# Feed-forward tiles in pairs, with their last passes on 64 rows each

## The chip, the core and the metric

The kernel runs on one core of a Trainium2 chip. The metric is the device time of one execution in microseconds, the median over several runs. The engines of the core are named as in the profile: PE multiplies matrices (PEld is its loading of weights), ACT applies functions, DVE and POOL do elementwise work, and SP issues most DMAs.

## The reference

The reference is one transformer block with modulated layer normalization, for 2048 tokens of 448 features in fp32: windowed attention with 16 heads, then a feed-forward network with the Mish function. Cut to what matters here:

```
h = _layernorm(x, axis=-1) * (1 + ca) + sa
x = x + ga * _A_ref(h, A_wqkv, A_wo)          # attention, window 256
h = _layernorm(x, axis=-1) * (1 + cb) + sb
x = x + gb * _B_ref(h, B_w1, B_b1, B_w2)

def _B_ref(x, w1, b1, w2):                    # w1: 448 x 1792, w2: 1792 x 448
    h = jnp.einsum("bsd,df->bsf", x, w1) + b1
    sp = jnp.log1p(jnp.exp(-jnp.abs(h))) + jnp.where(h > 0, h, jnp.zeros_like(h))
    act = h * jnp.tanh(sp)
    return jnp.einsum("bsf,fd->bsd", act, w2)
```

## The kernel before

The tokens are worked in four groups of 512 (NG = 4, GT = 512). Matmuls take fp32r operands, which PE streams faster than fp32 but with fewer bits. To keep precision each operand is split into a high part, rounded to fp32r, and a low part, the rest: `hh` and `hl` for the normalized input, `w13` and `w1l` for the first layer's weights, `ah` and `al` for the activations, `w2h` and `w2l` for the second layer's weights. A product is then high times high, high times low and low times high.

The 448 input features of the first layer are four chunks of partitions, three of 128 and one of 64. `passes` (L210) lists the matmuls of one output tile: three for each full chunk, and two for the last. In the last chunk the 64 features stand twice, on partitions 0 to 63 and again on 64 to 127 (`dup`, L222, copies them before the transposition). Its weights `w13[:, 3]` have the high part on partitions 0 to 63 and the low part on 64 to 127 (`split_lo`, L195, writes it there). So the tenth pass, `hh[:, 3]` with `w13[:, 3]`, makes high times high and high times low at once. The eleventh, `hl[:, 3]` with `w13[:, 3]`, makes low times high and, on the other 64 rows, low times low.

The feed-forward has 14 tiles of 128 hidden features (NF = 14) in each group, so n counts 56 tiles (NN). `f1_mm(n)` (L907) writes the 128 x 512 tile `z` in one PSUM bank with 11 passes of 512 columns. `f1_act(n)` (L917) makes t = Mish(z + b1) on ACT (L921), its high part `ah` on ACT (L922) and its low part `al` on DVE (L923). `ff2(n)` (L1091) multiplies them with the second layer's weights: for each of four token tiles three matmuls of 448 columns into one of four `acc` banks, 12 in all. After the 14th tile of a group it multiplies each bank with the gate on DVE (L1104), adds the residual (L1107) and stores the rows on SP.

The eight PSUM banks are two for `z`, four for `acc` and two for `tr`, which the transpositions of the next group's normalization use. `ftile` (L902) gives `ah` and `al` two buffers each and `t` one, in the pool `p1`. The pool `ff` holds the second layer's weights and the tiles that come in during the feed-forward.

The order is written out by hand in the loop of L1134. In round n it issues the passes and the activation of tile n, then `ff2(n - 1)`, so the second layer runs one tile behind the first. Tiles 0 and 1 are issued before the loop, in the attention's tail. `fill_step` (L1129) stands before and after `ff2`: it moves other work on by a step, first the rest of the attention's output and then, from the third tile of a group on, the normalization and transposition of the next group (`gen_x1_ln2`, L1110). In group 0 `pieces(n)` (L887) also splits the weights that come in. Before a new group starts, the rest of the fill work is issued.

Of the kernel before, what the change touches and what calls it, by code (L numbers as in the profile page):

```python
# [8 lines left out]
F32 = mybir.dt.float32  # L9
F32R = mybir.dt.float32r  # L10
# [5 lines left out]
NG, GT = 4, 512  # L16
NF = F // 128
# [34 lines left out]
def adaln_block(ctx: ExitStack, tc: tile.TileContext, x, wqkv, wo, w1, b1, w2, c, w_mod, out):  # L52
    nc = tc.nc
    PE, ACT, DVE, POOL = nc.tensor, nc.scalar, nc.vector, nc.gpsimd
# [3 lines left out]
    def dma(o, i):  # L58
        nc.sync.dma_start(o, i)

    def pool(name, side="left", space=None):
        kw = {} if space is None else {"space": space}
        cm = tc.tile_pool(name=name, bufs=1, reuse_waits="tile", side=side, **kw)
        st = ExitStack()
        return st.enter_context(cm), st
# [25 lines left out]
    def bank(tag, bufs, name):  # L91
        return PS[0].tile([128, 512], F32, name=name, tag=tag, bufs=bufs)
# [18 lines left out]
    for k in range(4):  # L111
        wmf = st0.tile([128, 2 * D], F32, name=f"wm01_{k}")
        t = wmf[0:112]
# [11 lines left out]
    for part in range(3):  # L125
        for ci in range(4):
            r0, r1 = ci * 128, min(ci * 128 + 128, D)
            for h in ((slice(0, 128),) if ci < 3 else (slice(0, 64), slice(64, 128))):
                t = wqs[ci][h]
# [80 lines left out]
    def passes(xh, xl, wh, wl):  # L210
        r = []
        for ci in range(3):
            r += [(xh[:, ci], wh[:, ci]), (xh[:, ci], wl[:, ci]), (xl[:, ci], wh[:, ci])]
        return r + [(xh[:, 3], wh[:, 3]), (xl[:, 3], wh[:, 3])]
# [48 lines left out]
    def new_T(key, pl):  # L263
        return (pl.tile([128, 4, GT], F32R, name=f"hh{key}", tag="hh"),
                pl.tile([128, 4, GT], F32R, name=f"hl{key}", tag="hl"))
# [59 lines left out]
    def flush():  # L325
        while later:
            later.pop(0)()
# [123 lines left out]
    hh, hl = HT[0] = new_T(0, mid)  # L451
# [67 lines left out]
    for i in range(2):  # L519
        t = att.tile([128, GT], F32, name=f"o2_{i}")  # L520
# [5 lines left out]
    def xr_tile(name):  # L526
        return mid.tile([128, 512], F32, name=name, tag="xr", bufs=3)
# [254 lines left out]
    FW = {}  # L782
    w2h, w2l, w2p, h2, x1 = {}, {}, {}, {}, {}
# [22 lines left out]
    def w1_hi(n):  # L806
        ci, c0 = W1[n]
        split_hi(w1p[n], FW["w13"][:, ci, c0:c0 + D], ACT)

    def w1_lo(n, eng):  # L810
        ci, c0 = W1[n]
        split_lo(w1p[n], FW["w13"][:, ci, c0:c0 + D], FW["w1l"][:, min(ci, 2), c0:c0 + D], ci, eng)
# [4 lines left out]
    def piece_load(i):  # L817
        if i < len(SEQ):
            (w2_dma if SEQ[i][0] == "w2" else w1_load)(SEQ[i][1])
# [58 lines left out]
    def w2_split(f):  # L878
        n = NF - 1 - f
        pl = FW["p1"] if f == 0 else FW["ff"]  # L880
        w2h[f] = (mid.tile([128, D], F32R, name=f"w2h{f}", tag="wo", bufs=7) if n < 7 else
                  pl.tile([128, D], F32R, name=f"w2h{f}"))
        w2l[f] = pl.tile([128, D], F32R, name=f"w2l{f}")
        ACT.activation(w2h[f], w2p[f], AF.Copy)
        (DVE if f < 1 else POOL).tensor_tensor(w2l[f], w2p[f], w2h[f].bitcast(F32), op=ALU.subtract)

    def pieces(f):  # L887
        for i, (kind, n) in enumerate(SEQ):
            if kind == "w2" and n == f:
                w2_split(n)  # L890
            elif kind == "w1" and (n - 4) // 2 == f:
                w1_hi(n)
                w1_lo(n, DVE if f < 1 else POOL)
            else:
                continue
            if "ff" in FW:
                piece_load(i + 6)

    NN = NG * NF
    ah, al, acc = {}, {}, {}  # L900

    def ftile(nm, n, dt=F32):  # L902
        return FW["p1"].tile([128, GT], dt, name=f"{nm}{n}", tag=nm, bufs=1 if nm == "t" else 2)

    zb = {}

    def f1_mm(n, tag, part=(0, 11)):  # L907
        g, f = divmod(n, NF)
        hh, hl = h2[g]
        fs = slice(f * 128, (f + 1) * 128)  # L910
        if part[0] == 0:
            zb[n] = bank(tag, 2, f"z{n}")
        ps = passes(hh, hl, FW["w13"][:, :, fs], FW["w1l"][:, :, fs])
        for m in range(*part):
            PE.matmul(zb[n], ps[m][1], ps[m][0], start=(m == 0), stop=(m == 10))  # L915

    def f1_act(n):  # L917
        f = n % NF
        ah[n], al[n] = ftile("ah", n, F32R), ftile("al", n, F32R)
        t = ftile("t", n)  # L920
        ACT.activation(t, zb[n], AF.Mish, bias=FW["b1c"][:, f:f + 1])  # L921
        ACT.activation(ah[n], t, AF.Copy)  # L922
        DVE.tensor_tensor(al[n], t, ah[n].bitcast(F32), op=ALU.subtract)  # L923
# [105 lines left out]
    for u in range(NU + 9):  # L1029
        s, k = divmod(u, 3)  # L1030
        g = s // H
# [12 lines left out]
        a = s + LEAD  # L1044
# [42 lines left out]
    ff, ff_s = pool("ff")  # L1087
    FW["ff"] = ff
    p1 = FW["p1"]

    def ff2(n):  # L1091
        g, f = divmod(n, NF)
        if f == 0:
            acc[g] = [bank("acc", 4, f"acc{g}_{t}") for t in range(4)]
        for t in range(4):
            ts = slice(t * 128, (t + 1) * 128)
            p = acc[g][t][:, 0:D]
            PE.matmul(p, ah[n][:, ts], w2h[f], start=(f == 0), stop=False)  # L1098
            PE.matmul(p, ah[n][:, ts], w2l[f], start=False, stop=False)  # L1099
            PE.matmul(p, al[n][:, ts], w2h[f], start=False, stop=(f == NF - 1))  # L1100
            if f == NF - 1:
                j = 4 * g + t
                y = xr_tile(f"yo{j}")[:, 0:D]
                DVE.tensor_tensor(y, p, gbn, op=ALU.mult)  # L1104
                for eng, a, b in (((DVE, 0, D),) if g < NG - 1 else ((POOL, 0, D),) if t < 3 else
                                  ((DVE, 0, 256), (POOL, 256, D))):
                    eng.tensor_tensor(y[:, a:b], y[:, a:b], x1[g][:, t, a:b], op=ALU.add)  # L1107
                dma(of[j * 128:(j + 1) * 128, :], y)

    def gen_x1_ln2(g):  # L1110
        if g > 1:
            x1_load(g, (ff, p1)[g % 2])
            yield
            yield
            yield

        def xn_tiles():
            t = mid.tile([128, 4, 512], F32, name=f"xn2_{g}", tag="on")
            return [t[:, i] for i in range(4)]
        yield from gen_ln2(g, ff, xn_tiles, "tr", 2)  # L1120
# [8 lines left out]
    def fill_step():  # L1129
        if fill is not None:  # L1130
            pipe.step()
            next(fill, None)
            flush()
    for n in range(NN + 1):  # L1134
        g, f = divmod(n, NF)
        if f == 0 and n:
            while fill is not None and next(fill, "END") != "END":
                pipe.step()
            fill = None
            while pipe.items:  # L1140
                pipe.step()
        if f == 2 and 0 < g < NG - 1:
            fill = gen_x1_ln2(g + 1)
        if 2 <= n < NN:
            f1_mm(n, "z")
            f1_act(n)
        if 0 < n < NF:
            pieces(n)
        if n:
            if n > 1:  # L1150
                fill_step()
            ff2(n - 1)
            for _ in range(1 + (g == 0) + (n == 1)):
                fill_step()
    for st in (ff_s, mid_s, cst_s, FW["s"], edge_s, psf_s):
        st.close()

# [22 lines left out]
```

## Time and profile before

| | |
|---|---|
| median of 3 runs | 718.31 us (717.83 to 719.37) |
| profiled execution | 719.96 us |
| its span on the core | 718.2 us |
| mean granted PE clock | 0.99 |
| matmul share of the span | 97% (4049 matmuls) |
| weight loads | 83% |
| DVE, ACT, POOL | 53%, 54%, 46% |
| first passes of z / last passes start | 414.4 us / 706.2 us |

Times in profile rows are microseconds from the start of the span. A row of the timeline has the start, the duration, the engine, the line, the operation, output and inputs with buffer numbers left out, and the count; what stands in brackets is idle time before it and who ended it. In a matmul's shape, 128*60 means weights of 128 rows (partitions) and 60 columns. The recorded duration of a matmul is longer than the distance to the next one, since matmuls are pipelined. So the distance between starts is what a matmul costs in a stream. A row that groups instructions has, behind the bar, the busy time in us and the mean duration in ns, then the idle time before them. A row of windows has the stretch, its length, and the busy time of the engine in it, then the granted clock, the DMA share and GB/s.

### The profile page before, as it was taken

What the parts mean: (1) busy time and instruction counts of PE and PEld (TensorE: products, weight loads), DVE (VectorE), ACT (ScalarE), POOL (GpSimd) and SP (SyncE); (2) the same over time, 40 slices, a digit from 0 to 9 for tenths busy, and PEclk for the clock granted to TensorE, in tenths of its full rate; (3) what the DMA queues carried; (4) which work ended last, traced back from release to release, by engine and by line L of the source; (5) the groups of instructions that cost most, each with busy time, mean ns of one, the idle gap of its engine ahead of it and who ended that gap; (6) DMA issues with size and microseconds to landing.
All of it is one profiled execution on the core that took longest, in us unless ns stands there. A gap on an engine that the chain in (4) does not pass through costs nothing.

```text
span 718.2 us, 12057 instructions
## 1 busy us (share of the span) xinstructions
PE 694.9 (97%) x4049; PEld 597.3 (83%) x4049; DVE 380.0 (53%) x1018; ACT 390.9 (54%) x740; POOL 327.0 (46%) x358
## 2 busy tenths in 40 slices
PE   8999999999999999999999899999999999999996
PEld 8777878788898888898887688888888888888885
DVE  5688657788555878656768642434323232322112
ACT  4538778768766768767868774243224222422221
POOL 6636778676666767666869744422010000000002
PEclk9999999999999999999999899999999999999999
DMA  7865763453761653744672165400200020001001
GB/s 215 257 211 178 251 204 122 148 158 125 212 207 50 203 166 88 230 137 137 216 223 75 52 216 157 116 1 2 102 1 1 4 99 1 0 7 45 0 1 51
DMA packets 48249, 83.86 MB, mean 117 GB/s; under 512 B 6142, under 2 KB 26348, under 8 KB 48188
## 3 DMA queue, kind: packets, MB, share of 16 engines
q1 hardware_dynamic: 47724, 83.10, 37.1%
q8 instruction: 32, 0.52, 0.3%
q14 instruction: 29, 0.24, 0.1%
q10 hardware_dynamic: 464, 0.00, 0.0%
HBM read 53.45 MB, written 29.36 MB: 115 GB/s over the span
## 4 chain that ended last, share of the span: by engine, by line
PE 72%; issue 11%; DVE 8%; DMA 4%; ACT 2%; POOL 1%; SPq 1%; POOLq 0%; DVEq 0%; ACTq 0%
PE z L915 15%; PE pv L740 9%; PE qk L314 8%; PE sA L678 5%; PE acc L1098 5%; PE acc L1100 5%; PE acc L1099 5%; PE sB L708 5%; PE wo L314 4%; PE qk_v L314 4%; PE sB L719 3%; DVE junk L680 3%; PE et L754 2%; DMA q<-mr 1%; DMA scr<-st 1%
## 5 line engine op out<-in xcount | busy, mean ns | idle before, releaser
L730 POOL TENSOR_TENSOR Pl<-P,Ph 128x512 fp32r<-128x512 f32 (+2 forms) x192 | 234.5, 1229 | 87.1 <-ACT Ph L723 49.4
L680 DVE CUSTOM_DVE_ANT_0 junk<-sA,mask 128x384 f32<-128x384 f32 (+2 forms) x256 | 135.2, 528 | 97.8 <-PE sA L678 89.5
L722 ACT ACTIVATE P<-sB 128x512 f32<-128x512 f32 (+2 forms) x192 | 109.8, 572 | 66.9 <-PE sB L719 61.7
L923 DVE TENSOR_TENSOR al<-t,ah 128x512 fp32r<-128x512 f32 x56 | 38.7, 692 | 199.7 <-ACT ah L922 199.7
L921 ACT ACTIVATE t<-z,b1c 128x512 f32<-128x512 f32 x56 | 38.5, 688 | 188.8 <-PE z L915 181.6
L723 ACT ACTIVATE Ph<-sB 128x512 fp32r<-128x512 f32 (+2 forms) x192 | 109.2, 569 | 0.0
L678 PE MATMUL sA<-k,q 84*128 84x384 f32 (+2 forms) x256 | 100.9, 396 | 2.2 <-DVE mx L680 1.5
L915 PE MATMUL z<-hhf,w 128*128 128x512 f32 x224 | 89.6, 400 | 0.0
L915 PE MATMUL z<-hlf,w 128*128 128x512 f32 x224 | 88.4, 395 | 0.0
L1098 PE MATMUL acc<-w2h,ah 128*128 128x448 f32 x224 | 82.0, 366 | 0.0
L1100 PE MATMUL acc<-w2h,al 128*128 128x448 f32 x224 | 81.7, 365 | 0.0
L1099 PE MATMUL acc<-w2l,ah 128*128 128x448 f32 x224 | 81.4, 364 | 0.0
L740 PE MATMUL pv<-Ph,v 128*60 128x256 f32 (+2 forms) x352 | 77.6, 295 | 3.6 <-DVE o L748 2.3
L740 PE MATMUL pv<-Pl,v 128*60 128x256 f32 (+2 forms) x352 | 74.4, 286 | 2.3 <-POOL Pl L730 2.3
L708 PE MATMUL sB<-q,k 86*128 86x256 f32 (+1 forms) x352 | 74.7, 286 | 1.4 <-DMA q<-mr 1.4
L915 PE MATMUL z<-hhf,w1l 128*128 128x512 f32 x168 | 66.3, 395 | 0.0
L708 PEld LDWEIGHTS sB<-q,k 86*128 86x128 f32 x352 | 62.4, 191 | 2.9 <-issue 1.2
L740 PEld LDWEIGHTS pv<-Ph,v 128*60 128x60 f32 x352 | 46.0, 135 | 18.0 <-ACT o L746 3.2
L719 PE MATMUL sB<-fdmask,identr 128*128 128x128 bf16 (+1 forms) x320 | 60.6, 255 | 0.0
L678 PEld LDWEIGHTS sA<-k,q 84*128 84x128 f32 x256 | 48.9, 192 | 8.5 <-DVE mx L680 5.9
L740 PEld LDWEIGHTS pv<-Pl,v 128*60 128x60 f32 x352 | 45.7, 133 | 11.0 <-POOL Pl L730 3.9
L1107 POOL TENSOR_TENSOR yo<-yo,x 128x448 f32<-128x448 f32 (+1 forms) x4 | 4.2, 1064 | 108.1 <-DVE yo L1104 108.1
(156 smaller groups left out, 1300.4 us busy)
## 6 DMA issues: line engine op xcount, KB each, us to landing
scr<-st SPq DMA_DIRECT2D x24, 512.0 KB
k<-scr SPq DMA_DIRECT2D x48, 252.0 KB
q<-scr SPq DMA_DIRECT2D x64, 168.0 KB
scr<-st SPq DMA_DIRECT2D x32, 256.0 KB
x<-x1d SPq DMA_DIRECT2D x10, 448.0 KB
xin<-in_A_x_dram SPq DMA_DIRECT2D x8, 448.0 KB
xr<-in_A_x_dram SPq DMA_DIRECT2D x16, 224.0 KB
x1d<-xr SPq DMA_DIRECT2D x16, 224.0 KB
```

Of the source, the lines that this page charges most:

```text
L314: PE.matmul(p, b, a, start=(n == 0), stop=(n == 10))
L678: PE.matmul(p[:, c0:384], q[0:84, t * 128:(t + 1) * 128], k[0:84, t * 128 + c0:t * 128 + 384], start=True, stop=True)
L680: DVE.tensor_tensor_reduce(out=junk[:, c0:384], in0=p[:, c0:384], in1=mask[:, c0:384], scale=1.0, scalar=-3.0e38, op0=ALU.add, op1=ALU.max ...
L708: PE.matmul(p[:, c:c + 128 * (t1 - t0)], k[:, jj * 128:(jj + 1) * 128], q[:, t0 * 128:t1 * 128], start=(n == 0), stop=False, skip_group_ch ...
L722: ACT.activation(P[:, c0:], p[:, c0:], AF.Exp, scale=SCALE)
L723: ACT.activation(Ph[u][:, c0:], p[:, c0:], AF.Exp, scale=SCALE)
L730: eng.tensor_tensor(Pl[u][:, a:b], Pt[u][:, a:b], Ph[u][:, a:b].bitcast(F32), op=ALU.subtract)
L740: PE.matmul(pv[0:60, t0 * 128:t1 * 128], V[j % NV][:, h, :], P[u][:, c:c + 128 * (t1 - t0)], start=(P is Ph and b == 0 and n == 0), stop=F ...
L915: PE.matmul(zb[n], ps[m][1], ps[m][0], start=(m == 0), stop=(m == 10))
L1098: PE.matmul(p, ah[n][:, ts], w2h[f], start=(f == 0), stop=False)
L1099: PE.matmul(p, ah[n][:, ts], w2l[f], start=False, stop=False)
L1100: PE.matmul(p, al[n][:, ts], w2h[f], start=False, stop=(f == NF - 1))
```

## The change

Group 0 keeps its order. In groups 1 to 3 the tiles are taken two at a time. `f1_pair(n)` issues the first ten passes of tile n and the first ten of tile n + 1, and then one matmul of 64 rows for each in place of the eleventh pass: `hl[0:64, 3]` with the high weights on partitions 0 to 63 for tile n, and `hl[64:128, 3]` with a copy of the high weights on partitions 64 to 127 for tile n + 1. They write different PSUM banks and use different halves of the array's rows. The term low times low of the last 64 features is no longer in the sum for these groups. Then come both activations, and after them the second layer of the two tiles of the round before, each with its fill steps.

The copy `w1x` is a new tile of 128 x 7 x 128 in the pool `ff`; one DMA on SP fills its partitions 64 to 127 with the high weights of the seven odd tiles, after group 0's last round is issued. `ftile` takes every second pair's `ah`, `al` and `t` from the pool `ff`, so there are four buffers of `ah` and `al` and two of `t` in all.

```diff
     def ftile(nm, n, dt=F32):
-        return FW["p1"].tile([128, GT], dt, name=f"{nm}{n}", tag=nm, bufs=1 if nm == "t" else 2)
+        pl = FW["ff"] if n >= NF and n // 2 % 2 else FW["p1"]
+        return pl.tile([128, GT], dt, name=f"{nm}{n}", tag=nm, bufs=1 if nm == "t" else 2)
...
-    for n in range(NN + 1):
+    w1x = ff.tile([128, NF // 2, 128], F32R, name="w1x")
+
+    def f1_pair(n):
+        hh, hl = h2[n // NF]
+        for m in (n, n + 1):
+            f1_mm(m, "z", (0, 10))
+        f = n % NF
+        PE.matmul(zb[n], FW["w13"][0:64, 3, f * 128:(f + 1) * 128], hl[0:64, 3], start=False, stop=True)
+        PE.matmul(zb[n + 1], w1x[64:128, f // 2], hl[64:128, 3], start=False, stop=True)
+        for m in (n, n + 1):
+            f1_act(m)
+
+    for n in range(NF):
+        if 2 <= n:
+            f1_mm(n, "z")
+            f1_act(n)
+        if n:
+            pieces(n)
+            if n > 1:
+                fill_step()
+            ff2(n - 1)
+            for _ in range(2 + (n == 1)):
+                fill_step()
+    odd = FW["w13"][0:64, 3].rearrange("p (a b c) -> p a b c", b=2, c=128)[:, :, 1]
+    dma(w1x[64:128].bitcast(F32), odd.bitcast(F32))
+    last = [NF - 1]
+    for n in range(NF, NN + 2, 2):
         g, f = divmod(n, NF)
-        if f == 0 and n:
+        if f == 0:
             while fill is not None and next(fill, "END") != "END":
                 pipe.step()
             fill = None
             while pipe.items:
                 pipe.step()
-        if f == 2 and 0 < g < NG - 1:
+        if f == 2 and g < NG - 1:
             fill = gen_x1_ln2(g + 1)
-        if 2 <= n < NN:
-            f1_mm(n, "z")
-            f1_act(n)
-        if 0 < n < NF:
-            pieces(n)
-        if n:
-            if n > 1:
-                fill_step()
-            ff2(n - 1)
-            for _ in range(1 + (g == 0) + (n == 1)):
-                fill_step()
+        if n < NN:
+            f1_pair(n)
+        for m in last:
+            fill_step()
+            ff2(m)
+            fill_step()
+        last = [n, n + 1]
```

## The prediction

> **What bounds the kernel now.** I read the page first (busy shares, the chain), then the matmul timeline of the feed-forward, then single rows for the prices.
>
> ```profile
> span 718.2 us, 12057 instructions
> PE 694.9 (97%) x4049; PEld 597.3 (83%) x4049; DVE 380.0 (53%) x1018; ACT 390.9 (54%) x740; POOL 327.0 (46%) x358
> ...
> PE z L915 15%; PE pv L740 9%; PE qk L314 8%; PE sA L678 5%; PE acc L1098 5%; PE acc L1100 5%; PE acc L1099 5%; PE sB L708 5%; PE wo L314 4%; PE qk_v L314 4%; PE sB L719 3%; DVE junk L680 3%; PE et L754 2%; DMA q<-mr 1%; DMA scr<-st 1%
> ```
>
> Matmul is busy nearly always, and the chain that ended last runs through the lines of the feed-forward. A busy matmul record is not a proof (each is longer than the distance to the next), so the stretch in which the last three groups run has to be looked at by itself.
>
> ```profile
> 494.00:704.00 210.00, 210.00 (x986) 1.00 0.06 23
> ...
> 703.91 0.39 PE L915 MATMUL z<-hhf,w 128*128 128x512 f32 x1
> 704.15 0.39 PE L915 MATMUL z<-hhf,w1l 128*128 128x512 f32 x1
> ...
> 706.01 0.39 PE L915 MATMUL z<-hhf,w 128*128 128x512 f32 x1
> 706.24 0.39 PE L915 MATMUL z<-hlf,w 128*128 128x512 f32 x1
> 706.47 0.37 PE L1098 MATMUL acc<-w2h,ah 128*128 128x448 f32 x1
> 706.67 0.36 PE L1099 MATMUL acc<-w2l,ah 128*128 128x448 f32 x1
> ...
> 711.15 0.36 PE L1100 MATMUL acc<-w2h,al 128*128 128x448 f32 x1
> ```
>
> In the window of 210 us the matmul rows fill all 210 at a granted clock of 1.00, with DMA at 6%. The eleven passes of one z tile run from 703.91 to 706.47: (706.47 - 703.91) / 11 = 0.233 us a pass, whether it is the first or the low-part pass at 706.24. The second layer's matmuls stand 0.20 us apart (706.67 - 706.47, 448 columns). Both give about 0.455 ns a column, with nothing left for a gap. So here the end is set by the sum of the matmul distances, and what the change takes from or adds to that sum comes out at the end. Behind the last matmul at 711.15 some 7 us of output work follow, which the change leaves alone.
>
> **The change part by part.** The last three groups have 42 z tiles, which become 21 pairs. In each pair 20 passes stay. The two low-part passes, 2 x 0.233 = 0.466 us, become two matmuls of 64 rows, one on partitions 0 to 63 and one on 64 to 127, each with 512 columns. If I call the lateness of the second half behind the first d, and the price of changing between 128 rows and 64 rows s (paid on the way in and on the way out), a pair costs 0.233 + d + 2s in place of 0.466. The gain or loss is 21 times the difference.
>
> No matmul of 64 rows is in the trace, so both unknowns are bounded by the nearest rows. For **s** there is one place where the number of rows falls below 64, the transposition of the bias with 14 rows, and a transposition with 128 rows beside which it can be held; PE had been idle before both.
>
> ```profile
> 362.63 0.37 PE L314 MATMUL wo<-wo,hlo 128*128 128x448 f32 x1
> 362.93 0.13 PEld L842 LDWEIGHTS b1t<-ident,b1r 14*128 14x128 f32 x1 [0.31 <-DVE mv L220]
> 362.93 0.23 PE L842 MATMUL b1t<-ident,b1r 14*128 14x14 f32 x1
> 363.09 0.19 PEld L678 LDWEIGHTS sA<-k,q 84*128 84x128 f32 x1
> 363.09 0.44 PE L678 MATMUL sA<-k,q 84*128 84x384 f32 x1
> 363.19 0.31 PEld L740 LDWEIGHTS pv<-Ph,v 128*60 128x60 f32 x2
> ```
>
> ```profile
> 61.03 0.08 PEld L686 LDWEIGHTS mt<-ident,mx 128*8 128x8 f32 x1 [0.65 <-DVE mx L680]
> 61.03 0.27 PE L686 MATMUL mt<-ident,mx 128*8 128x128 f32 x1 [0.50 <-DVE mx L680]
> 61.04 0.13 PEld L740 LDWEIGHTS pv<-Ph,v 128*60 128x60 f32 x1
> 61.15 0.13 PEld L740 LDWEIGHTS pv<-Pl,v 128*60 128x60 f32 x1
> ```
>
> In the stream a weight load begins when the matmul ahead of it begins. Behind the 128-row transposition the next load began 0.01 us after it (61.04), and the one after that, which marks the start of the next matmul, 0.12 us after it (61.15). Of these 0.12, 128 columns at 0.455 ns are 0.06, which leaves about 0.06 for its own load. Behind the 14-row one the next load was held until 0.16 us after its start, and the matmul started 0.10 later still (363.19). Its own load and 14 columns were over by 0.06 + 0.01 = 0.07, so the next matmul started 0.26 - 0.07 = 0.19 us after the array had its last column, where the stream shows nothing: 0.09 of holding, 0.10 of a load that nothing covers. That is one sample, and a semaphore could have held the second matmul, since a maximum over an earlier sA tile was just ending on DVE (362.49 + 0.53 = 363.02):
>
> ```profile
> 362.49 0.53 DVE L680 CUSTOM_DVE_ANT_0 junk<-sA,mask 128x384 f32<-128x384 f32 x1
> ```
>
>  Bounds: s = 0, if the hold was that; and 0.26, if an engine waits for the recorded end of a pass (0.39 - 0.233 = 0.16 behind its last column) and loads after it (0.10). I take 0.19, the row that is nearest in kind.
>
> The Trainium skill, TensorEngine Tiling (Array Packing), section Key Properties, says that a change of the tiling mode, unlike a change of tile within a mode, drains the engine; it gives no time for that. By it s cannot be 0, and the 14-row row agrees as I read it, with 0.19.
>
> For **d**, if the second half's load begins as the first half's matmul begins, as all loads in the stream do, the second matmul starts one uncovered load later. Such a load shows where the z passes follow the short transpositions:
>
> ```profile
> 607.80 0.60 PE L249 MATMUL trf<-ident,xn 128*128 128x128 f32 x4
> 608.16 0.48 PE L915 MATMUL z<-hhf,w 128*128 128x512 f32 x1
> 608.48 0.39 PE L915 MATMUL z<-hhf,w1l 128*128 128x512 f32 x1
> ```
>
> The first pass takes 0.32 where 0.233 is usual, so 0.09 for the load; the bias row has 0.10. If both loads run side by side, d is 0. I take the middle, d = 0.05, since no row shows loads to different rows. Should the halves not run together at all, d is a whole pass, 0.233.
>
> The sum: 0.233 + 0.05 + 2 x 0.19 = 0.663 against 0.466, so 0.197 more in a pair and 21 x 0.197 = **4.1 us more**. Its ends are 21 x (-0.233) = -4.9 (s and d nothing) and 21 x (0.10 + 0.52 - 0.233) = +8.1.
>
> The Trainium skill, TensorE: Matmul & The Clock Gate, section Part 3: Packing small matmuls, has matmuls in distinct row groups run at once, starting some 4 ns apart. With that figure as d, an estimate with s = 0.19 is 21 x (0.004 + 0.38 - 0.233) = +3.2; no run here shows it yet.
>
> **What is moved and costs nothing**, with its cover:
>
> ```profile
> L921 ACT ACTIVATE t<-z,b1c 128x512 f32<-128x512 f32 x56 | 38.5, 688 | 188.8 <-PE z L915 181.6
> L922 ACT ACTIVATE ah<-t 128x512 fp32r<-128x512 f32 x52 | 32.9, 632 | 1.7
> L923 DVE TENSOR_TENSOR al<-t,ah 128x512 fp32r<-128x512 f32 x56 | 38.7, 692 | 199.7 <-ACT ah L922 199.7
> ...
> L1104 DVE TENSOR_TENSOR yo<-acc,gbn 128x448 f32<-128x448 f32 x16 | 9.9, 619 | 3.0 <-DMA out_dram<-yo 2.1 <-PE acc L1100 1.0
> ```
>
> Both activations now come behind the pair's last matmul, and the second waits for the first's al, since t has one buffer in each pool. That is 0.69 + 0.63 + 0.69 = 2.0 us for the first tile, 4.0 for both, and the second z bank is free after 2.7. The second layer of the pair before (24 x 0.20 = 4.9 us) covers that, and its own second layer comes only after the next pair's passes; without this cover a pair would wait up to 4 us. In the last round, where no passes follow, the first tile has 4.9 us for its 2.0. Where a group ends, the four acc banks wait for DVE's products and sums, eight of some 0.62 us, while two tiles of passes (4.9) now run in place of one; that is safer than before. The steps of the next group's normalization stand at the same count beside each second layer.
>
> The copy of the odd tiles' weights is one DMA of 64 partitions x 7 x 512 bytes = 0.23 MB on SP. Its neighbours there, with the start of group 1's first tile between them:
>
> ```profile
> 464.83 0.33 SPq L59 DMA_DIRECT2D w2p<-in_B_w_dram  x1
> ...
> 495.76 0.39 PE L915 MATMUL z<-hhf,w 128*128 128x512 f32 x1
> ...
> 501.81 3.92 SPq L59 DMA_DIRECT2D out_dram<-yo  x4
> ```
>
> SP issues nothing for 37 us in between. The first pair needs the copy some 4.7 us after its start near 495.8, and the weights were split long before. If it did come late, the wait would fall on one pair, not on 21.
>
> **The rivals.** *Cheap switching*: the array changes its rows without holding loads, s = 0, and the halves run together. For it speaks that only one row of the trace shows a hold, with DVE's end on sA just before it; against it the 0.19 itself. With d from 0 to 0.10 it gains 21 x 0.133 to 21 x 0.233, 2.8 to 4.9 us, so 713.4 to 715.5, middle 714.5: faster. It decides below the point where 2s + d = 0.233, with d = 0.05 that is s = 0.09. Of the Trainium skill, Part 3 of TensorE: Matmul & The Clock Gate speaks for it, Key Properties of TensorEngine Tiling (Array Packing) against it.
>
> *Half-hidden switching*: the next weights load during the hold, so s is only the larger of 0.09 and 0.10. Then 21 x (0.20 + 0.05 - 0.233) = +0.4, 718.7. The 363.09 row speaks against it, because the load began only after the hold.
>
> *The change doesn't do what it says*: the halves run one after the other, as all matmuls of the trace do. Without a price for the change of rows nothing is gained, 718.3; with s = 0.19 it is 21 x 0.38 = +8.0, 726.3.
>
> **How the numbers follow.** The profiled execution took 719.96 us, span 718.2 and 1.8 around it, which is 1.65 above the median of 718.31 (717.83 to 719.37). The terms are differences of PE time, so I set them on the median: 718.3 + 4.1 = **722.4 us**. Chances: forecast 0.43, cheap switching 0.31, half-hidden 0.14, one after the other 0.12 (0.04 without, 0.08 with a price). A measurement tells 0.2%, 1.4 us, from no change. Faster: 0.31 + 0.02 of half-hidden = 0.33; same: 0.09 + 0.04 = 0.13; slower: 0.43 + 0.03 + 0.08 = 0.54. The forecast's own range, s from 0.15 to 0.23 and d from 0 to 0.10, is 21 x 0.067 to 21 x 0.327, so 719.7 to 725.2. The range over the cases reaches from cheap switching's 713.4 to 724.5, and leaves out the dear end of the serial case and thin tails.
>
> **What would show it.** In the timeline of a pair: the distance from the last 128-row pass of z to the first 64-row matmul (0.233 means no price on the way in), from one half to the other (d), and from the second half to the first second-layer matmul (0.233 means no price on the way out; I expect some 0.42). The rest of the passes should stand 0.233 and 0.20 apart as now, and no matmul of the groups should wait for ACT, DVE or the copy. The forecast is wrong if the two halves stand together and the next matmuls follow one pass later.

## The result, and the profile after

The changed kernel takes 726.84 us (median of 4 runs, 725.56 to 727.38) against 718.49 us of before beside it. The ratio is 1.0113 with a 95% interval of 1.0095 to 1.013, so it is 8.4 us slower. I had forecast slower, but by 4.1 us, and the time lies above my range (713.4 to 724.5).

From the page of the changed kernel its span and busy shares, and one row of windows:

```profile
span 725.6 us, 12028 instructions
PE 697.4 (96%) x4049; PEld 589.3 (81%) x4049; DVE 380.8 (52%) x1018; ACT 391.0 (54%) x740; POOL 326.4 (45%) x358
...
494.00:704.00 210.00, 205.47 (x944) 168.57 (x943) 58.43 (x91) 58.42 (x88) 6.15 (x13) 1.00 0.06 23
```

The last line is the same stretch of 210 us as before, now with all engines (PE, PEld, DVE, ACT, POOL). Matmul no longer fills it: 205.5 of 210 us, at the same granted clock of 1.00. So there are real gaps in a stretch that had none.

The stage gives the amount without the scatter of the attention ahead of it. From the first matmul of group 1 to the last of the second layer it took 711.15 - 495.76 = 215.39 us before. Now it takes 718.64 - 494.35 = 224.29, which is 8.90 more. The first rows to read are those that the prediction named, one pair's last passes. This is the timeline of the changed kernel, matmuls and weight loads (start, duration, engine, line):

```profile
708.00 0.39 PE L916 MATMUL z<-hlf,w 128*128 128x512 f32 x1
708.00 0.19 PEld L916 LDWEIGHTS z<-hhf,w 128*128 128x128 f32 x1
708.23 0.40 PE L916 MATMUL z<-hhf,w 128*128 128x512 f32 x1
708.55 0.18 PEld L1142 LDWEIGHTS z<-hlf,w 64*128 64x128 f32 x1 [0.36 <-issue]
708.56 0.49 PE L1142 MATMUL z<-hlf,w 64*128 64x512 f32 x1
708.56 0.18 PEld L1143 LDWEIGHTS z<-hlf,w1x 64*128 64x128 f32 x1
708.56 0.50 PE L1143 MATMUL z<-hlf,w1x 64*128 64x512 f32 x1
708.99 0.19 PEld L1099 LDWEIGHTS acc<-w2h,ah 128*128 128x128 f32 x1 [0.25 <-issue]
708.99 0.48 PE L1099 MATMUL acc<-w2h,ah 128*128 128x448 f32 x1
...
709.10 0.19 PEld L1100 LDWEIGHTS acc<-w2l,ah 128*128 128x128 f32 x1
709.30 0.36 PE L1100 MATMUL acc<-w2l,ah 128*128 128x448 f32 x1
```

The two halves start together (708.56 both) and so do their loads. But neither load began while the pass before it ran, as the other loads of the stream do (the pass at 708.23 has its load at 708.00). The last 128-row pass starts at 708.23 and needs 0.233 for its columns; the loads begin only 0.32 later, so they were held for 0.09. The second layer's first load is held in the same way behind the 64-row matmuls (708.56 to 708.99 = 0.43: 0.11 for the load, 0.233 for the columns, 0.09 of holding). Its own 0.11 (708.99 to 709.10) is uncovered too.

From the pass at 708.23 to the second layer's second matmul at 709.30 it is 1.07 us. Before, the same four distances were 3 x 0.233 + 0.20 = 0.90. So a pair costs 0.16 to 0.17 more, and 21 pairs some 3.4 us. That is less than half of what was lost. The rest stands where the next group's normalized tile is transposed, in the changed kernel between second-layer matmuls:

```profile
530.04 0.49 PE L249 MATMUL trf<-ident,xn 128*128 128x128 f32 x3
532.33 0.33 PE L249 MATMUL trf<-ident,xn 128*128 128x128 f32 x1 [1.80 <-DVE xn L240]
534.93 0.60 PE L249 MATMUL trf<-ident,xn 128*128 128x128 f32 x4
...
546.58 0.63 PE L249 MATMUL trf<-ident,xn 128*128 128x128 f32 x4 [0.46 <-DVE hlf L261]
```

A bracket on PE, of which the groups had none before: the fourth transposition of the first chunk waits 1.80 us for its input from DVE, and the last chunk 0.46 us for a PSUM bank that DVE reads. Group 2 has the same two waits (1.82 and 0.46). What DVE and ACT did in that time, in the changed kernel's timeline:

```profile
527.61 0.69 ACT L922 ACTIVATE t<-z,b1c 128x512 f32<-128x512 f32 x1 [6.58 <-PE z L1143]
528.33 0.63 ACT L923 ACTIVATE ah<-t 128x512 fp32r<-128x512 f32 x1
528.99 0.69 DVE L924 TENSOR_TENSOR al<-t,ah 128x512 fp32r<-128x512 f32 x1 [5.97 <-ACT ah L923]
529.78 0.69 ACT L922 ACTIVATE t<-z,b1c 128x512 f32<-128x512 f32 x1 [0.82 <-DVE al L924]
530.50 0.63 ACT L923 ACTIVATE ah<-t 128x512 fp32r<-128x512 f32 x1
531.16 0.69 DVE L924 TENSOR_TENSOR al<-t,ah 128x512 fp32r<-128x512 f32 x1 [1.48 <-ACT ah L923]
531.77 0.51 DVE L240 TENSOR_SCALAR xn<-x,mv,rsf 128x448 f32<-128x448 f32 x1
```

Both tiles of a pair end with its last matmuls, so both activations start only then (527.61). The second waits 0.82 for t. The normalized row tile (531.77) stands behind both al in DVE's order of work, 4.2 us after the activations could start; DVE was idle for 1.48 us ahead of the second al and did not start it earlier. One tile's second layer takes 2.45 us, and the transposition stands behind the first of the two. In the kernel before, the row tile stands behind one al only:

```profile
528.40 0.69 ACT L921 ACTIVATE t<-z,b1c 128x512 f32<-128x512 f32 x1 [3.62 <-PE z L915]
529.79 0.69 DVE L923 TENSOR_TENSOR al<-t,ah 128x512 fp32r<-128x512 f32 x1 [3.44 <-ACT ah L922]
530.40 0.51 DVE L240 TENSOR_SCALAR xn<-x,mv,rsf 128x448 f32<-128x448 f32 x1
530.61 0.68 PE L249 MATMUL trf<-ident,xn 128*128 128x128 f32 x4
```

There it is ready at 530.91, while the four transpositions that start at 530.61 are still running.

How much these waits cost follows from the distances between pairs. In group 1 of the changed kernel three rounds with four chunks took from 522.31 to 557.21 = 34.90 us, where three usual rounds of 10.14 are 30.42: 4.48 more. Before, five rounds with the same four chunks took from 525.65 to 552.50 = 26.85, where five of 4.985 are 24.93: 1.93 more. The difference is 2.55 us a group, 5.1 for two groups. With 3.4 that is 8.5 of the stage's 8.9; the kernels in pairs below bear on the other 0.4.

### The profile page after: what moved, and what is told of

Its sections match the earlier page's. It is cut to its first block, busy times and chain, and to the rows that moved or that the text cites. A ratio compares the mean times of both kernels' runs of the same rounds, so it can differ in the third digit from the quotient of the medians.

```text
span 725.6 us, 12028 instructions
## 1 busy us (share of the span) xinstructions
PE 697.4 (96%) x4049; PEld 589.3 (81%) x4049; DVE 380.8 (52%) x1018; ACT 391.0 (54%) x740; POOL 326.4 (45%) x358
## 4 chain that ended last, share of the span: by engine, by line
PE 67%; issue 11%; DVE 9%; ACT 5%; POOL 1%; DMA 1%; POOLq 0%; DVEq 0%; ACTq 0%
PE z L916 15%; PE pv L740 9%; PE qk L314 8%; PE sA L678 5%; PE sB L708 4%; PE acc L1099 4%; PE wo L314 4%; PE acc L1101 4%; PE acc L1100 4%; PE qk_v L314 4%; PE sB L719 3%; DVE junk L680 3%; PE et L754 2%; ACT P L722 1%; ACT t L922 1%
## 5 line engine op out<-in xcount | busy, mean ns | idle before, releaser
L916 PE MATMUL z<-hhf,w 128*128 128x512 f32 x224 | 86.0, 399 | 0.0
L1099 PE MATMUL acc<-w2h,ah 128*128 128x448 f32 x224 | 84.5, 377 | 0.0
L916 PE MATMUL z<-hlf,w 128*128 128x512 f32 x182 | 71.9, 395 | 0.0
```

## The experiments

Each ratio is to the kernel before on the same chip, and us are differences of medians or, where said, of the stage.

**Pairs with full passes** (full_asis). Only the 64-row matmuls were undone:

```diff
         for m in (n, n + 1):
-            f1_mm(m, "z", (0, 10))
-        f = n % NF
-        PE.matmul(zb[n], FW["w13"][0:64, 3, ...], hl[0:64, 3], start=False, stop=True)
-        PE.matmul(zb[n + 1], w1x[64:128, f // 2], hl[64:128, 3], start=False, stop=True)
+            f1_mm(m, "z")
```

> Pairs, but with all eleven 128-row passes for each tile, so no 64-row matmul and no change of rows. Theory A (two causes: about 3.4 us from the change between 128 and 64 rows, 21 pairs of 0.16 us, and about 4.9 us from transpositions that wait behind both activations of a pair): only the second is left, so 718.5 + 4.9 = 723.4 us. Theory B (the whole 8.3 us comes with the 64-row matmuls): 718.5 us.

Measured: 718.35 us against 717.94, ratio 1.0005 (0.9995 to 1.0014). Theory A expected 4.9 us over before, the kernel took 0.4, and theory B looked right. The timeline of ACT in this kernel shows why it was not yet a test of A:

```profile
523.82 0.69 ACT L922 ACTIVATE t<-z,b1c 128x512 f32<-128x512 f32 x1 [6.03 <-PE z L916]
524.54 0.63 ACT L923 ACTIVATE ah<-t 128x512 fp32r<-128x512 f32 x1
526.38 0.69 ACT L922 ACTIVATE t<-z,b1c 128x512 f32<-128x512 f32 x1 [1.21 <-PE z L916]
```

With full passes tile n ends 2.57 us before tile n + 1, so the two activations stand 2.56 apart (523.82, 526.38). The changed kernel moves two things at once: the number of rows, and the end of the pair's first tile. I changed theory A into A': the wait comes from that late end, not from the pairs as such.

**Full passes, with both last ones at the end** (late_asis). No 64-row matmul, but the eleventh passes stand where the change has its last passes (the edit is shown against full_asis):

```diff
-        for m in (n, n + 1):
-            f1_mm(m, "z")
+        for part in ((0, 10), (10, 11)):
+            for m in (n, n + 1):
+                f1_mm(m, "z", part)
```

> Full 128-row passes in pairs, but with the eleventh pass of both tiles at the pair's end, as the 64-row ones stand in the changed kernel; the normalization is where the change has it. Theory A' (the transpositions' wait comes from the first tile of a pair ending 2.3 us later, so that both activations start together and DVE's work for the transpositions is behind them): about 4.9 us over before, 722.9 us, with matmul idle before the transpositions as in the changed kernel. Theory C (the wait comes with the 64-row matmuls themselves): 718.3 us.

Measured: 722.82 us against 717.64, ratio 1.0073 (1.0046 to 1.0101), 5.2 us more; in the stage 713.84 - 492.87 = 220.97, 5.6 more. The waits are those of the changed kernel:

```profile
530.20 0.33 PE L249 MATMUL trf<-ident,xn 128*128 128x128 f32 x1 [1.77 <-DVE xn L240]
...
544.24 0.63 PE L249 MATMUL trf<-ident,xn 128*128 128x128 f32 x4 [0.44 <-DVE hlf L261]
```

So the wait needs no 64-row matmul. It needs only that both tiles end together.

**The normalization moved** (half_moved, and full_moved with full passes). An extra step at the start brings the last row tile into the round before, and an extra step of the delayed work at each round's end brings DVE's evacuation ahead of the next activations:

```diff
             fill = gen_x1_ln2(g + 1)
+            fill_step()
...
             fill_step()
+        pipe.step()
         last = [n, n + 1]
```

> The changed kernel with the normalization of the next group moved: one extra step when it starts, and one more step of the delayed work at the end of each round. Theory A: the waits of the transpositions (about 2.45 us in each of two groups) go, 726.8 - 4.9 = 721.9 us, and the 0.16 us a pair stay. Theory B: 726.8 us.

Measured: 721.04 us, ratio 1.0042 (1.0024 to 1.0061), 3.1 us over before where 3.4 was expected. No transposition has a DVE bracket left:

```profile
529.28 0.66 PE L249 MATMUL trf<-ident,xn 128*128 128x128 f32 x4
532.20 0.60 PE L249 MATMUL trf<-ident,xn 128*128 128x128 f32 x4
540.26 0.66 PE L249 MATMUL trf<-ident,xn 128*128 128x128 f32 x4
543.16 0.60 PE L249 MATMUL trf<-ident,xn 128*128 128x128 f32 x4
```

> Both undone: eleven 128-row passes in pairs, and the normalization moved. Theory A: nothing is left of the two costs, 718.5 us (718 to 719). If pairing itself has a third cost, it shows here as time above 718.5.

Measured: 718.44 us, ratio 1.0005 (0.9993 to 1.0017). Pairs, buffers and the copy of weights have no cost that the medians can tell from nothing. In the stage the three kernels in pairs without 64-row matmuls and without waits (full_asis, full_moved, and rows96_moved below) take 215.87, 215.79 and 215.82 us, where the one trace of before has 215.39. These 0.4 to 0.5 are about what is missing between 8.5 and 8.9; where they come from stays open.

**Both matmuls on one half** (same_half), which tells whether the halves run at once or only look so in the records:

```diff
-        PE.matmul(zb[n + 1], w1x[64:128, f // 2], hl[64:128, 3], start=False, stop=True)
+        PE.matmul(zb[n + 1], FW["w13"][0:64, 3, (f + 1) * 128:(f + 2) * 128], hl[0:64, 3], start=False, stop=True)
```

> The changed kernel, but both 64-row matmuls take partitions 0 to 63 (weights and input of the same half). Theory A with halves that run at once (second starts 0.01 us after the first): here the second must follow the first, 21 x 0.23 = 4.9 us more, 731.7 us. If the records only look concurrent, because ends of matmuls are modelled, nothing changes: 726.8 us.

Measured: 730.83 us, ratio 1.0176 (1.0161 to 1.0191). That is 0.0063 above the changed kernel's ratio, 4.5 us. Its timeline:

```profile
561.51 0.39 PE L916 MATMUL z<-hhf,w 128*128 128x512 f32 x1
561.83 0.50 PE L1142 MATMUL z<-hlf,w 64*128 64x512 f32 x1
561.94 0.19 PEld L1143 LDWEIGHTS z<-hlf,w 64*128 64x128 f32 x1
562.17 0.39 PE L1143 MATMUL z<-hlf,w 64*128 64x512 f32 x1
562.49 0.47 PE L1099 MATMUL acc<-w2h,ah 128*128 128x448 f32 x1
562.80 0.37 PE L1100 MATMUL acc<-w2l,ah 128*128 128x448 f32 x1
```

From 561.51 to 562.80 it is 1.29, where the changed kernel has 1.07: 0.22 more, one pass, 4.6 us for 21 pairs. The two waits of the transpositions are some 0.23 us shorter each (1.58 and 0.23 in group 1), since tile n ends a pass earlier, so the stage, 721.50 - 493.28 = 228.22, is only 3.9 longer than the changed kernel's. The halves do run at once, and the pass that they save is real. The distances to and from the 64-row matmuls are the same, so the price belongs to the change of rows and not to the pair of halves.

**One 64-row matmul for each tile, in the order of before** (single). It leaves out low times low in groups 1 to 3, as the changed kernel does:

```diff
-            f1_mm(n, "z")
+            f1_mm(n, "z", (0, 11 if g == 0 else 10))
+            if g:
+                PE.matmul(zb[n], FW["w13"][0:64, 3, f * 128:(f + 1) * 128], h2[g][1][0:64, 3], start=False, stop=True)
             f1_act(n)
```

> The order of before, with one 64-row matmul as each tile's eleventh pass in groups 1 to 3: 42 changes to 64 rows and back, and no second half beside it. If a change there and back costs 0.40 us wherever it stands (0.09 before it, 0.20 and 0.11 behind it), 42 x 0.40 = 16.7 us: 734.6 us. If the price belongs to the pair of halves, less than half of that.

Measured: 734.27 us against 717.64, 16.6 more, ratio 1.0226 (1.0202 to 1.0251). One of its 42 places:

```profile
563.39 0.39 PE L915 MATMUL z<-hhf,w 128*128 128x512 f32 x1
563.71 0.49 PE L1147 MATMUL z<-hlf,w 64*128 64x512 f32 x1
564.13 0.47 PE L1098 MATMUL acc<-w2h,ah 128*128 128x448 f32 x1
564.44 0.36 PE L1099 MATMUL acc<-w2l,ah 128*128 128x448 f32 x1
```

The distances 0.32, 0.42 and 0.31 against 0.233, 0.233 and 0.20 are 0.38 to 0.39 a place. 42 of them are 16.2 us, and the stage has 726.44 - 495.04 = 231.40, which is 16.0 more.

**96 rows** (rows96_moved), as half_moved with `hl[0:96, 3]` and `w13[0:96, 3]` for each tile:

> As half_moved, but the two last passes take 96 rows each (partitions 0 to 95), one after the other. If only 64 rows or fewer make the array change, they stand 0.233 us apart like all others and the time is before's, 717.9 (to 718.6) us. If any change in the number of rows is charged, 717.9 + 21 x 0.40 = 726.3 us.

Measured: 718.13 us against 717.64, ratio 1.0012 (0.9995 to 1.0029). The two passes in its timeline, merged in one row, stand like all others (566.67 - 566.20 = 2 x 0.235):

```profile
565.97 0.39 PE L916 MATMUL z<-hhf,w 128*128 128x512 f32 x1
566.20 0.63 PE L1144 MATMUL z<-hlf,w 96*128 96x512 f32 x2
566.67 0.37 PE L1099 MATMUL acc<-w2h,ah 128*128 128x448 f32 x1
```

So 96 rows cost nothing, and 64 do. Where between 64 and 96 it begins was not tried. The attention's 84 rows stand without a hold: in the kernel before, the load behind the 84-row matmul at 364.18 begins at 364.26, and the next matmul at 364.44, which is 0.18 later and no more than its 384 columns at 0.455 ns.

**t in turn from two pools** (t_alt), which shortens the block of activations without moving a matmul:

```diff
-        pl = FW["ff"] if n >= NF and n // 2 % 2 else FW["p1"]
+        pl = FW["ff"] if n >= NF and (n if nm == "t" else n // 2) % 2 else FW["p1"]
```

> The changed kernel with t taken from the two pools in turn by tile and not by pair, so that the second activation of a pair need not wait for the first tile's al (0.82 us in the changed kernel). If the transpositions wait for DVE's work behind that block, each first wait shrinks by 0.8 us (1.8 to 1.0) and the second (0.46) goes: 2 x 1.28 = 2.6 us less than the changed kernel, so 5.8 us over before in place of 8.4. The 64-row distances (0.33, 0.43, 0.31) stay. If the block has nothing to do with it, 8.4 us over before.

Measured: 722.45 us against 716.94, 5.5 more where 5.8 was expected, ratio 1.0083 (1.0054 to 1.0112). In the stage it is 713.70 - 492.60 = 221.10, 3.2 less than the changed kernel where 2.6 less was expected. The ratio's interval touches that of the changed kernel, so the rows carry the verdict:

```profile
528.29 0.49 PE L249 MATMUL trf<-ident,xn 128*128 128x128 f32 x3
529.66 0.33 PE L249 MATMUL trf<-ident,xn 128*128 128x128 f32 x1 [0.88 <-DVE xn L240]
```

The first wait fell from 1.80 to 0.88, and the last chunk has no bracket any more.

**The 64-row matmuls first in the pair** (half_first; the cut leaves out the definition of `f1_late` and the two matmuls taken from the pair's end):

```diff
+        for m in (n, n + 1):
+            zb[m] = bank("z", 2, f"z{m}")
+        PE.matmul(zb[n], FW["w13"][0:64, 3, f * 128:(f + 1) * 128], hl[0:64, 3], start=True, stop=False)
+        PE.matmul(zb[n + 1], w1x[64:128, f // 2], hl[64:128, 3], start=True, stop=False)
         for m in (n, n + 1):
-            f1_mm(m, "z", (0, 10))
...
+            f1_late(m)            # the ten 128-row passes, start=False
```

> The changed kernel with the two 64-row matmuls as the first of a pair in place of the last; the normalization is where the change has it. Theory A': tile n ends 2.3 us ahead of tile n + 1, the transpositions wait no more, and only the price of the change of rows is left, 21 x 0.16 = 3.4 us: 721.4 us. Theory C: 726.3 us, as the changed kernel.

Measured: 723.72 us against 717.64, 6.1 more, ratio 1.0077 (1.0054 to 1.01). Theory A' missed by 2.7 us here. The transpositions wait no more, but the very first pair found a new wait, on the low part of the last chunk, which is made last and was now needed first:

```profile
494.70 0.36 PE L1101 MATMUL acc<-w2h,al 128*128 128x448 f32 x1
496.25 0.49 PE L1149 MATMUL z<-hlf,w 64*128 64x512 f32 x1 [1.18 <-DVE hlf L261]
```

That place costs 1.2 us, once. From the end of the matmul at 494.70 (0.20 later) to the last one at 715.17 the stage is 220.27, 4.9 over before: 3.4 of the price and this 1.2 account for 4.6 of it. The remaining 1.2 of the median's difference lies ahead of this stage, in the attention, or in the scatter; the interval (3.9 to 7.2 us) allows it. That part stays open.

No run beat the kernel before. With the measured 0.39 for a change there and back and 0.22 for a further pass of 64 rows, four tiles at one change would cost 0.39 + 0.233 + 0.22 = 0.84 where four passes are 0.93. That estimate, 0.09 us for four tiles, needs four z banks and was not tried.

## Why the prediction was wrong

The direction and the first mechanism held; the amount did not, since one step was put at nothing.

**The change of rows: right, with d too dear.** I took s = 0.19 from one row with 14 rows, one sample which a semaphore could have explained. The runs show 0.39 there and back, so s is just under 0.20, in all 21 or 42 places, and a load held and then uncovered, as that row had it. For d I took 0.05 and it is 0.00 to 0.01. So the sum for 21 pairs is some 3.4 where I had 4.1. The Trainium skill says in TensorEngine Tiling (Array Packing), Key Properties, that a change of mode drains the engine; the 0.09 of holding on each side agrees. The Trainium skill's 4 ns between the starts, in TensorE: Matmul & The Clock Gate, Part 3, agree with two starts that the rows put at most 0.01 us apart.

**The rivals.** Cheap switching fell with the rows 708.23 to 708.56; single has 0.39 at each of 42 places. Half-hidden switching fell too, as the loads began after the hold. That the halves run one after the other fell with same_half, which is that case and costs 4.5 us more. My 726.3 for it is near the measured time, for a reason that is not its own.

**What is moved and costs nothing: wrong.** "The steps of the next group's normalization stand at the same count beside each second layer." The count was right, and the 4.0 us that I worked out for both activations were nearly so (4.2, from 527.61 to 531.85). I held these 4.0 against the second layers of the pair before, which is the wait of z and of the pair's own second layer. I did not hold them against the other work that stands behind them on DVE: the row tile that a transposition needs after one second layer, 2.45 us, and the evacuation that frees a bank. A late transposition also holds what stands behind it on PE: the second layer's next matmul came only at 532.41, behind the transposition at 532.33. Before, a tile's al was alone ahead of that work and left it in time (530.91). The sign that the prediction named, that no matmul of the groups waits for DVE, failed in the rows 532.33 and 546.58. Late_asis shows the wait without 64 rows, half_moved shows the 64 rows without the wait, and t_alt shows that the wait follows the length of the block. It is 5.1 us by the rounds, 5.2 in late_asis.

**The sum** should have been 3.4 + 5.1 = 8.5 against 8.4 measured. The range failed with the same step: its upper part was made from s and d alone. It even stopped at 724.5, short of the 725.2 that the forecast's own s and d allowed, but the measured time lies above both.

**The rest held.** The copy of the weights never shows as a wait, the passes stand 0.233 and 0.20 apart, and the tail did not change.

## What to carry to other kernels

Two matmuls of 64 rows on both halves of the array run in the time of one, but each change between 128 and 64 rows cost 0.20 us here, 0.09 of holding and 0.11 of a load that was not made ahead. By these figures it pays only where a stay in 64 rows saves more than 0.39 us, an estimated two 512-column passes or more (2 x 0.233). When two tiles are made to end together, their evacuations become one block: look for all that stands behind that block on each in-order engine, not only for the tiles' own consumers. When an experiment undoes one part of a change, see whether it moves another part back unmeant, as the full passes in pairs did with the late end.

## What the runs showed of the hardware

A matmul of 96 rows streams like one of 128 (0.235 apart in rows96_moved) while one of 64 rows is held on both sides by 0.09 us and has its 0.11 us load uncovered. Two loads for different halves of the array begin together (708.55 and 708.56) and do not add up: the next load comes 0.43 later, as behind a single 64-row matmul (0.42). With both on one half, the second 64-row matmul follows 0.34 after the first, which is the first one's load of 0.11 and its columns of 0.233. The second's own load (561.94) runs under them, so it costs 0.22 more in all. At a granted clock of 1.00 the distances of the changed kernel repeated within 0.02 us in all 21 pairs.
